# Turning a slot's rows on VectorE instead of TensorE, in a fused attention and mixture-of-experts kernel

## The chip, the cores and the metric

The kernel runs on one core of a Trainium2 chip, in float32 throughout. The metric is the device time of one execution in microseconds (us); lower is better. The program is one launch: attention, routing and the expert layers follow each other and overlap inside it.

## The reference, cut to what matters

The reference computes sliding-window attention (8 batches, 8 heads, 576 positions, head size 64; half of the heads use a dilated window), turns the result into 4608 token rows of 512 numbers, and passes them through a mixture of 8 experts. Each token goes to the one expert with the highest gate value.

```python
x = np.ascontiguousarray(attn_out.transpose(0, 2, 1, 3)).reshape(B * S, H * D)   # 4608 x 512
logits = x @ w_gate                                                              # 512 x 8
expert_idx = np.argmax(logits, axis=1)
...
for e in range(E):
    lo, hi = (boundaries[e], boundaries[e + 1])
    h = np.maximum(x_sorted[lo:hi] @ w1[e], 0.0)       # w1[e]: 512 x 1024
    y_sorted[lo:hi] = h @ w2[e]                        # w2[e]: 1024 x 512
y = y_sorted[inv_perm]
return (gate_w[:, None] * y).astype(np.float32)
```

Only the sum over the 512 features of a row enters `x @ w1`, so the order in which the features lie on the 128 partitions is free, as long as a row and `w1` use the same order.

## The kernel before, in words

**Two streams of work.** `attention()` walks over 32 units (batch, kind of window, half of the heads). When a batch is finished, `route(b)` picks an expert for each of its tokens and scatters the rows (512 features, the gate value and the token's number: `ROW` = 514 floats) into a bucket per expert in DRAM. `moe()` walks over slots. A slot is 128 rows of one expert; it reads them back from the bucket and runs both expert layers on them. There are up to `NSLOT` = 41 slots, of which the first `SURE` = 36 always run; each later one stands behind a condition (`guards`, `tc.If(live[0] > j)`). In this data slots 0 to 36 do their work. Slots 26 and 29 are mixed: their 128 rows come in four groups of 32, some of one expert and some of another, and they run through `grouped` and `hrow`.

**Order.** Both streams are generators. A planner (`run_slots`, `clock`) interleaves their pieces by estimated costs, so that slots run between attention units as soon as enough batches are routed. From about 490 us on only slots are left, apart from the last routing. The framework keeps each engine's queue in order; `tc.issue_after` ties an instruction behind another one.

**One slot.** `fetch_x(j)` reads a register with the slot's place in the bucket (`queue.value_load`) and loads the 128 rows into the tile `x` (128 partitions by 514 floats, four buffers) with one DMA of 257 KB. For slots below 26 this goes through SyncE's queue (SP), from 26 on through ScalarE's (ACT), where it is tied behind the slot's first relu (`evicted[-1]`) while `j < SURE`. `fetch_w` loads four quarters of 1 MB (two halves of `w1`, two of `w2`) on SP into one of two sets of weight buffers, by the parity of the slot; a quarter is skipped when the expert has not changed. `fetch()` decides when each load is issued: its list `wanted` names how many halves of earlier slots must be done.

`across(j)` turns the rows: four 128 by 128 TensorE transposes (L1171) into one PSUM bank, and one VectorE copy to the SBUF tile `xt` (L1173). It is called for slot j+1 in the middle of slot j, between the two halves of the first layer. The first layer is 32 matmuls of 128 by 128 (L1239), each recorded as two matmul instructions, so 64 a slot; ScalarE applies the relu to the first half (L1250) and VectorE to the second (L1259). The second layer is 8 matmuls of 128 by 512 (L1271), recorded as 16; ScalarE scales the result by the gate value that lies in `x` (L1282), and POOL scatters it to the output (L1288).

A float32 row of `w1` numbered `128 c + l` lies on partition `l`, as chunk `c` of four.

Of the kernel before, what the change touches and what calls it, by code (L numbers as in the profile page):

```python
# [12 lines left out]
F32 = mybir.dt.float32  # L13
# [10 lines left out]
N, DM, E, F = B * S, H * DH, 8, 1024  # L24
# [12 lines left out]
ROW = DM + 2  # L37
G = 32
# [24 lines left out]
SURE = N // 128  # L63


READY = [max(0, -(-(S * (b + 1) - E * 127) // 128)) for b in range(B)]
# [9 lines left out]
MIX = (2, 5)  # L76
STEP = MIX[1] - MIX[0]
J0 = STAGES[-1][1]
assert J0 + MIX[-1] < SURE and NSLOT - SURE <= 6


# [82 lines left out]
def kernel(  # L164
# [10 lines left out]
    nc = tc.nc  # L175
# [53 lines left out]
    def read_bucket(i, b):  # L229

        i = getattr(i, "ins", i)
        for b2, w in bucket_writes:
            if b2 > b:
                tc.declare_no_dep(i, w, reason="writes rows that this stage does not read")
        tc.add_to_no_dep_group("reads", i)
# [14 lines left out]
    def bank(name, *dims):  # L250
        return psum.tile([128, *(dims or (512,))], F32, tag="bank", name=name)
# [819 lines left out]
    w1s = cpool.tile([128, 2, 4, F], F32, name="w1")  # L1071
    w2s = cpool.tile([128, 2, 8, DM], F32, name="w2")
    mixed = {J0 + at0: i for i, at0 in enumerate(MIX)}
    xs, guards, evicted = {}, ExitStack(), []

    def fetch_x(j):
        b, n, _, basei, _ = where[j]
        x = xs[j] = mpool.tile([128, ROW], F32, tag="x", name=f"x_{j}", bufs=4)
        with ExitStack() as order:


            queue = nc.sync
            if j >= J0 + 2:
                queue = nc.scalar
                if j < SURE:
                    order.enter_context(tc.issue_after(evicted[-1].ins))
            if j in mixed:
                for g in range(4):
                    a = 2 * NMIX + 4 * mixed[j] + g
                    at0 = queue.value_load(  # L1090
                        mix["ints"][:, a : a + 1], min_val=0, max_val=NROWS - G
                    )
                    read_bucket(queue.dma_start(x[G * g : G * g + G], bucket[ds(at0, G), :]), b)
            else:
                at0 = queue.value_load(basei[:, n : n + 1], min_val=0, max_val=E * CAP)
                read_bucket(queue.dma_start(x, bucket[ds(at0, 128), :]), b)

    regs = {}

    def fetch_w(j, dst, src, other):  # L1100
        _, n, exi, _, newi = where[j]
        if (j, other) not in regs:
            if other:
                i = mixed[j]
                exi = mix["ints"][:, i : i + 1]
                newi = mix["ints"][:, NMIX + i : NMIX + i + 1]
            else:
                exi, newi = exi[:, n : n + 1], newi[:, n : n + 1]
            rv = nc.sync.value_load(exi, min_val=0, max_val=E - 1)
            kw = {}  # L1110
            if j >= 2:
                kw["cond"] = nc.sync.value_load(newi, min_val=0, max_val=1) > 0
            regs[j, other] = rv, kw
        rv, kw = regs[j, other]
        nc.sync.dma_start(dst, src(rv).rearrange("o (c l) f -> l (o c) f", l=128), **kw)

# [22 lines left out]
    def fetch():  # L1141
        while wanted:

            at0 = 0
            while at0 < len(wanted) - 1 and wanted[at0][1] == "x" and wanted[at0][0] not in where:
                at0 += 1
            j, what, layer, n = wanted[at0]
            if j not in where or done[layer] < n:
                return
            wanted.pop(at0)  # L1150
            if what == "x":
                fetch_x(j)
                continue
            h, other = int(what[2]), what[3:] == "b"
            n = (j + other) % 2
            if what[1] == "1":
                cols = slice(512 * h, 512 * h + 512)
                fetch_w(j, w1s[:, n, :, cols], lambda rv: moe_w1[ds(rv, 1), :, cols], other)
            else:
                rows = slice(512 * h, 512 * h + 512)  # L1160
                fetch_w(
                    j, w2s[:, n, 4 * h : 4 * h + 4], lambda rv: moe_w2[ds(rv, 1), rows, :], other
                )

    def moe():


        def across(j):
            ps = bank("xt", 4, 128)
            for c in range(4):  # L1170
                nc.tensor.transpose(ps[:, c], xs[j][:, 128 * c : 128 * c + 128], ident)  # L1171
            xt = mpool.tile([128, 4, 128], F32, tag="xt", name="xt")
            crossed.append(nc.vector.tensor_copy(xt, ps))  # L1173
            return xt

        late, xt = [], None
        for j in range(NSLOT):
# [5 lines left out]
            if j >= SURE:  # L1183

                guards.close()
                guards.enter_context(tc.If(live[0] > j))
                while late:
                    late.pop(0)()
            x = xs[j]
# [7 lines left out]
            def grouped(out, lhsT, ws, cols, c, n, j=j):  # L1197

                for g in range(4):
                    mine = slice(G * g, G * g + G)  # L1200
                    nc.tensor.matmul(  # L1201
                        out[mine],
                        lhsT=lhsT[:, mine],
                        rhs=ws[:, (j + (g >= KIND[mixed[j]])) % 2, c, cols],
                        start=c == 0,
                        stop=c == n - 1,
                    )

            def turned_h(hrow, fg):
                ps = bank("ht", 4, 128)  # L1210
                for fi in range(4):
                    nc.tensor.transpose(ps[:, fi], hrow[:, fi], ident)
                (nc.scalar.copy, nc.vector.tensor_copy)[fg](h[:, 4 * fg : 4 * fg + 4], ps)

            hrows = []
            for fg in range(2) if j in mixed else ():
                ph = bank("ph")
                for c in range(4):
                    grouped(ph, xt[:, c], w1s, slice(512 * fg, 512 * fg + 512), c, 4)
                    if (fg, c) == (1, 1):  # L1220
                        turned_h(hrows[0], 0)
                    yield 0.93
                hrow = mpool.tile([128, 4, 128], F32, tag="xt", name="hrow")
                flat = hrow.rearrange("p i f -> p (i f)")
                done[0] = 2 * j + fg + 1
                if fg == 0:
                    evicted.append(nc.scalar.activation(flat, ph, AF.Relu))
                    while late:
                        late.pop(0)()
                else:  # L1230
                    relu = nc.vector.tensor_scalar(flat, ph, 0.0, None, op0=OP.max)
                fetch()
                hrows.append(hrow)
            for fg in range(2) if j not in mixed else ():
                ph = bank("ph", 4, 128)
                for fi in range(4):
                    f = 4 * fg + fi
                    for c in range(4):
                        nc.tensor.matmul(  # L1239
                            ph[:, fi],  # L1240
                            lhsT=w1[:, c, 128 * f : 128 * f + 128],
                            rhs=xt[:, c],
                            start=c == 0,
                            stop=c == 3,
                        )
                    if fi < 3:
                        yield 0.93
                done[0] = 2 * j + fg + 1
                if fg == 0:
                    evicted.append(nc.scalar.activation(h[:, 0:4], ph, AF.Relu))  # L1250
                    while late:
                        late.pop(0)()
                    fetch()
                    yield 0.93
                    if j + 1 in xs:
                        nxt = across(j + 1)
                        yield 0.5
                else:
                    relu = nc.vector.tensor_scalar(h[:, 4:8], ph, 0.0, None, op0=OP.max)  # L1259
                    fetch()  # L1260
                    yield 0.93
            py = bank("py")
            for f in range(8):
                if j in mixed:
                    if f == 2:
                        turned_h(hrows[1], 1)
                    if f == 4 and j + 1 in xs:
                        nxt = across(j + 1)
                    grouped(py, h[:, f], w2s, slice(0, DM), f, 8)
                else:  # L1270
                    nc.tensor.matmul(py, lhsT=h[:, f], rhs=w2[:, f], start=f == 0, stop=f == 7)  # L1271
                if f == 3:
                    done[1] = 2 * j + 1
                    fetch()
                if f < 7:
                    yield 0.88
# [117 lines left out]
```

## Time and profile before

| | |
|---|---|
| median of 3 runs | 775.67 us (774.82 to 775.92) |
| the profiled execution, its own time | 830.33 us |
| its span, first to last instruction | 828.5 us |
| mean granted TensorE clock in it | 0.956 |
| PE, DVE, ACT, POOL busy | 93%, 33%, 28%, 18% |
| HBM read and written | 216.16 MB and 21.54 MB |

The profile has five parts that are used here: the busy shares by slice, the chain of work that ended last, groups of instructions by line, the waits, and a timeline. PE is TensorE's matmul, PEld its weight load, DVE is VectorE, ACT is ScalarE, POOL is GpSimd and SP is SyncE; a q behind an engine's name is its queue of DMA issues. The profiled execution takes 54.66 us more than the median run. Its lines are used for what a piece of work costs and for what waits on what.

### The profile page before, as it was taken

The page shows a single profiled execution, that of the slowest core. Times are in us where ns is not written, and L with a number is a line of the kernel's source. Part 1 is how long each engine was busy: PE and PEld are TensorE (multiplying, and loading weights), DVE is VectorE, ACT ScalarE, POOL GpSimd, SP SyncE. Part 2 cuts the span into 40 slices and gives each one's busy share as a digit, 9 for nine tenths or more (in the row PEclk, how much of TensorE's full clock was granted, in tenths as well). Part 3 has the DMA queues.
Part 4 walks back from the last instruction along what each step waited for, and adds up shares of the span by engine and source line. Part 5 has one row for each costly group of instructions (what it writes and reads, how often), then busy time and mean ns, then how long its engine had stood idle before and what let it go on. Part 6 is the DMA issues. An engine that isn't in the chain of part 4 may idle for free.

```text
span 828.5 us, 18147 instructions
## 1 busy us (share of the span) xinstructions
PE 773.6 (93%) x6870; PEld 574.1 (69%) x6870; DVE 274.4 (33%) x963; ACT 229.1 (28%) x853; POOL 146.3 (18%) x142
## 2 busy tenths in 40 slices
PE   6997997998999899989999899969999999999993
PEld 4776775886777677767777677646777466577681
DVE  3674765664343433443341311135110110101010
ACT  4985663552333233222331010000100101000010
POOL 4424333113111311130110200060000000000000
PEclk9998979898999899998999989978999999999997
DMA  7985679998998968796406818978994292883996
GB/s 184 208 194 162 139 187 323 294 264 265 358 269 294 305 189 243 245 303 232 132 26 223 261 59 289 327 241 295 313 335 149 93 317 99 318 313 138 324 312 213
DMA packets 177053, 195.42 MB, mean 236 GB/s; under 512 B 71249, under 2 KB 103137, under 8 KB 176963
## 3 DMA queue, kind: packets, MB, share of 16 engines
q1 hardware_dynamic: 166960, 169.01, 65.8%
q0 software_dynamic: 7248, 21.43, 7.2%
q10 hardware_dynamic: 2754, 3.78, 1.4%
q8 instruction: 57, 0.93, 0.5%
q14 instruction: 34, 0.27, 0.1%
HBM read 216.16 MB, written 21.54 MB: 287 GB/s over the span
## 4 chain that ended last, share of the span: by engine, by line
PE 85%; issue 5%; ACT 5%; DVE 1%; another core or an unknown queue 1%; DMA 1%; POOLq 0%; ACTq 0%; POOL 0%; DVEq 0%
PE ph L1239 31%; PE py L1271 29%; PE xo L469 5%; PE weights L454 3%; PE scores L388 3%; ACT e L425 3%; PE turned L342 2%; PE xt L1171 2%; PE ph L1201 2%; PE py L1201 2%; PE logits L583 2%; PE xrow L573 2%; PE turned L351 2%; DMA k<-in_k_dram 1%
## 5 line engine op out<-in xcount | busy, mean ns | idle before, releaser
L1239 PE MATMUL ph<-xt,w 128*128 128x128 f32 x2240 | 276.4, 280 | 4.1 <-issue 3.1
L1239 PEld LDWEIGHTS ph<-xt,w 128*128 128x128 f32 x2240 | 267.3, 196 | 18.0 <-issue 15.7
L1271 PE MATMUL py<-w,h 128*128 128x512 f32 x560 | 262.5, 609 | 3.9 <-issue 3.9
L1271 PEld LDWEIGHTS py<-w,h 128*128 128x128 f32 x560 | 102.8, 194 | 107.9 <-issue 105.9
L1288 POOL DMA_INDIRECT out_dram<-y,to x35 | 34.8, 993 | 412.0 <-ACT y L1282 326.6
L1173 DVE COPY xt<-xt 128x512 f32<-128x512 f32 x38 | 26.3, 691 | 211.1 <-PE xt L1171 205.8
L1282 ACT ACTIVATE y<-py,x 128x512 f32<-128x512 f32 x35 | 24.0, 687 | 223.0 <-PE py L1271 181.4
L444 POOL TENSOR_TENSOR e<-e,rec 128x864 f32<-128x864 f32 x32 | 52.2, 1631 | 142.2 <-DVE rec L443 121.7
L456 DVE COPY eT<-weights 96x384 f32<-96x384 f32 x96 | 47.3, 545 | 58.6 <-PE weights L454 44.9
L469 PE MATMUL xo<-eT,v 96*64 96x64 f32 (+1 forms) x1216 | 51.6, 233 | 13.7 <-issue 13.6
L469 PEld LDWEIGHTS xo<-eT,v 96*64 96x64 f32 x1216 | 44.1, 144 | 21.0 <-issue 16.6
L425 ACT ACTIVATE e<-e,lo 128x96 f32<-128x96 f32 x144 | 51.8, 362 | 12.0 <-DVE lo L417 10.9
L425 ACT ACTIVATE e<-scores,lo 128x96 f32<-128x96 f32 (+1 forms) x160 | 52.4, 345 | 2.3 <-DVE lo L404 1.9
L239 POOL DMA_INDIRECT bucket<-rows,idx x40 | 39.0, 975 | 56.0 <-DVE idx L671 37.3
L1259 DVE TENSOR_SCALAR h<-ph 128x512 f32<-128x512 f32 x35 | 24.1, 688 | 73.5 <-PE ph L1239 73.5
L334 ACT COPY kT<-turned 128x288 f32<-128x288 f32 x64 | 22.5, 403 | 86.0 <-PE turned L342 44.0
L1250 ACT ACTIVATE h<-ph 128x512 f32<-128x512 f32 x35 | 20.9, 596 | 89.9 <-PE ph L1239 73.7
L454 PE MATMUL weights<-ident,e 128*96 128x128 f32 x288 | 39.3, 281 | 3.0 <-issue 2.0
L454 PEld LDWEIGHTS weights<-ident,e 128*96 128x96 f32 x288 | 32.2, 129 | 10.4 <-issue 8.1
L388 PEld LDWEIGHTS scores<-kT,qT 64*64 64x64 f32 x1152 | 31.8, 143 | 9.7 <-issue 4.0
L388 PE MATMUL scores<-kT,qT 64*64 64x96 f32 x1152 | 36.8, 260 | 1.2 <-ACT kT L334 1.0
L410 DVE TENSOR_TENSOR e<-scores,masks 128x384 f32<-128x384 f32 x64 | 23.0, 399 | 33.7 <-PE scores L388 18.1
(220 smaller groups left out, 612.5 us busy)
## 6 DMA issues: line engine op xcount, KB each, us to landing
w<-in_moe_w_dram SPq DMA_DIRECT2D x164, 1024.0 KB
x<-bucket SPq DMA_DIRECT2D x26, 257.0 KB
v<-in_v_dram SPq DMA_DIRECT2D x32, 192.0 KB
q<-in_q_dram SPq DMA_DIRECT2D x32, 144.0 KB
v<-in_v_dram SPq DMA_DIRECT2D x48, 96.0 KB
k<-in_k_dram SPq DMA_DIRECT2D x28, 144.0 KB
x<-bucket ACTq DMA_DIRECT2D x11, 257.0 KB
q<-in_q_dram SPq DMA_DIRECT2D x14, 192.0 KB
```

Source lines behind the costliest of these rows:

```text
L239: nc.gpsimd.indirect_dma_start(out=bucket, out_offset=bass.IndirectOffsetOnAxis(ap=idx, axis=0), in_=rows, in_offset=None, bounds_check=NR ...
L388: nc.tensor.matmul(sc[r][64 * c : 64 * c + 64, 96 * (i % 5) : 96 * (i % 5) + 96], lhsT=qT[rows, 64 * j : 64 * j + 64], rhs=kT[rows, first_ ...
L425: nc.scalar.activation(out=e[p0:p1, i], in_=s[:, 96 * (i - i0) : 96 * (i - i0) + 96], func=AF.Exp, bias=lo[p0:p1, i : i + 1], scale=-1.0, ...
L444: return nc.gpsimd.tensor_tensor(out=e, in0=e, in1=rec.unsqueeze(2).broadcast_to([128, 9, 96]), op=OP.mult)
L454: nc.tensor.transpose(tp[0:96, 128 * i : 128 * i + 128], e[:, a + i], ident)
L456: nc.vector.tensor_copy(eT, tp[0:96, 0:384])
L469: nc.tensor.matmul(xo[DH * h : DH * h + DH, at0 : at0 + nq], lhsT=vt[:, 2 * hl + r, j, :] if ty == 0 else vt[:, hl, j, DH * r : DH * r + D ...
L1173: crossed.append(nc.vector.tensor_copy(xt, ps))
L1201: nc.tensor.matmul(out[mine], lhsT=lhsT[:, mine], rhs=ws[:, (j + (g >= KIND[mixed[j]])) % 2, c, cols], start=c == 0, stop=c == n - 1,)
L1239: nc.tensor.matmul(ph[:, fi], lhsT=w1[:, c, 128 * f : 128 * f + 128], rhs=xt[:, c], start=c == 0, stop=c == 3,)
L1271: nc.tensor.matmul(py, lhsT=h[:, f], rhs=w2[:, f], start=f == 0, stop=f == 7)
L1288: i = nc.gpsimd.indirect_dma_start(out=out, out_offset=bass.IndirectOffsetOnAxis(ap=to, axis=0), in_=y, in_offset=None, bounds_check=N - 1 ...
```

## The change

From slot 11 on (`PIECES = READY[3]`, which is 11), except for the two mixed slots, the turning of the rows moves from TensorE to VectorE.

- [...] `fetch_x` brings the rows in four pieces: piece i holds features 128 i to 128 i + 127 of all 128 rows, and goes to partitions 32 i to 32 i + 31. In it, partition 32 i + t holds the features of rows t, 32 + t, 64 + t and 96 + t. A fifth DMA brings the last two columns (gate value and token number) in the old layout. One DMA of 128 runs of 2056 bytes becomes four of 128 runs of 512 bytes each and one of 128 runs of 8 bytes.
- `across` for these slots is one VectorE transpose of 128 by 512 from `x` to `xt`. It reads every fourth float (a step of 16 bytes) and needs neither TensorE nor a PSUM bank.
- The features then lie as `4 l + c` on partition l. All `w1` loads follow (`fetch_w` is passed the order "(l c)" for `w1` and "(c l)" for `w2`): partition l gets rows 4 l to 4 l + 3. Each run is still 512 floats long.
- For slots 0 to 10, 26 and 29 TensorE still turns the rows, but its weight load now also reads every fourth float of `x`. The copy to `xt` has a new order: `xt` is [128, group of 32 rows, c, row], and the first layer's matmul reads four runs of 32 floats.
- The ties of `x` loads behind the last relu now hold until the first guarded slot has begun (`guarded`), so for the loads of slots 36 and 37 too.

```diff
     def fetch_x(j):
...
+        pieces = j >= PIECES and j not in mixed
...
             if j >= J0 + 2:
                 queue = nc.scalar
-                if j < SURE:
+                if not guarded:
                     order.enter_context(tc.issue_after(evicted[-1].ins))
...
                 at0 = queue.value_load(basei[:, n : n + 1], min_val=0, max_val=E * CAP)
-                read_bucket(queue.dma_start(x, bucket[ds(at0, 128), :]), b)
+                rows = bucket[ds(at0, 128), :]
+                for i in range(4) if pieces else ():
+                    part = rows[:, 128 * i : 128 * i + 128].rearrange("(g t) d -> t g d", t=G)
+                    mine = x[G * i : G * i + G, 0:DM].rearrange("t (g d) -> t g d", g=4)
+                    read_bucket(queue.dma_start(mine, part), b)
+                skip = DM if pieces else 0
+                read_bucket(queue.dma_start(x[:, skip:ROW], rows[:, skip:ROW]), b)
...
-        nc.sync.dma_start(dst, src(rv).rearrange("o (c l) f -> l (o c) f", l=128), **kw)
+        nc.sync.dma_start(dst, src(rv).rearrange(f"o {rows} f -> l (o c) f", l=128), **kw)
...
         def across(j):
+            x = xs[j][:, 0:DM]
+            xt = mpool.tile([128, 4, 4, G], F32, tag="xt", name="xt")
+            if j >= PIECES and j not in mixed:
+                crossed.append(
+                    nc.vector.transpose(xt, x.rearrange("p (g d c) -> p g c d", g=4, c=4))
+                )
+                return xt
             ps = bank("xt", 4, 128)
             for c in range(4):
-                nc.tensor.transpose(ps[:, c], xs[j][:, 128 * c : 128 * c + 128], ident)
-            xt = mpool.tile([128, 4, 128], F32, tag="xt", name="xt")
-            crossed.append(nc.vector.tensor_copy(xt, ps))
+                nc.tensor.transpose(ps[:, c], x.rearrange("p (d c) -> p c d", c=4)[:, c], ident)
+            crossed.append(
+                nc.vector.tensor_copy(
+                    xt.rearrange("p g c t -> p c g t"), ps.rearrange("p c (g t) -> p c g t", g=4)
+                )
+            )
             return xt
...
             if j >= SURE:
                 guards.close()
                 guards.enter_context(tc.If(live[0] > j))
+                guarded.append(j)
...
                         nc.tensor.matmul(
-                            ph[:, fi],
+                            ph[:, fi].rearrange("p (g t) -> p g t", g=4),
                             lhsT=w1[:, c, 128 * f : 128 * f + 128],
-                            rhs=xt[:, c],
+                            rhs=xt[:, :, c],
```

More of the change, by code (lines that the diff above doesn't have):

```diff
@@ L78 @@
 J0 = STAGES[-1][1]
+PIECES = READY[3]
 assert J0 + MIX[-1] < SURE and NSLOT - SURE <= 6
@@ L1073 @@
     mixed = {J0 + at0: i for i, at0 in enumerate(MIX)}
-    xs, guards, evicted = {}, ExitStack(), []
+    xs, guards, guarded, evicted = {}, ExitStack(), [], []
     def fetch_x(j):
@@ L1095, in fetch_x, with fetch_w @@
                 at0 = queue.value_load(basei[:, n : n + 1], min_val=0, max_val=E * CAP)
-                read_bucket(queue.dma_start(x, bucket[ds(at0, 128), :]), b)
+                rows = bucket[ds(at0, 128), :]
[5 more added lines that the diff above has]
+                read_bucket(queue.dma_start(x[:, skip:ROW], rows[:, skip:ROW]), b)
     regs = {}
-    def fetch_w(j, dst, src, other):
+    def fetch_w(j, dst, src, other, rows):
         _, n, exi, _, newi = where[j]
@@ L1157, in fetch @@
                 cols = slice(512 * h, 512 * h + 512)
-                fetch_w(j, w1s[:, n, :, cols], lambda rv: moe_w1[ds(rv, 1), :, cols], other)
+                fetch_w(
+                    j, w1s[:, n, :, cols], lambda rv: moe_w1[ds(rv, 1), :, cols], other, "(l c)"
+                )
             else:
@@ L1161, in fetch @@
                 fetch_w(
-                    j, w2s[:, n, 4 * h : 4 * h + 4], lambda rv: moe_w2[ds(rv, 1), rows, :], other
+                    j,
+                    w2s[:, n, 4 * h : 4 * h + 4],
+                    lambda rv: moe_w2[ds(rv, 1), rows, :],
+                    other,
+                    "(c l)",
                 )
@@ L1168, in across @@
         def across(j):
+            x = xs[j][:, 0:DM]
[5 more added lines that the diff above has]
+                return xt
             ps = bank("xt", 4, 128)
             for c in range(4):
-                nc.tensor.transpose(ps[:, c], xs[j][:, 128 * c : 128 * c + 128], ident)
-            xt = mpool.tile([128, 4, 128], F32, tag="xt", name="xt")
-            crossed.append(nc.vector.tensor_copy(xt, ps))
+                nc.tensor.transpose(ps[:, c], x.rearrange("p (d c) -> p c d", c=4)[:, c], ident)
[3 more added lines that the diff above has]
+                )
+            )
             return xt
@@ L1202, in grouped @@
                         out[mine],
-                        lhsT=lhsT[:, mine],
+                        lhsT=lhsT(g),
                         rhs=ws[:, (j + (g >= KIND[mixed[j]])) % 2, c, cols],
@@ L1211, in turned_h @@
                 for fi in range(4):
-                    nc.tensor.transpose(ps[:, fi], hrow[:, fi], ident)
+                    nc.tensor.transpose(
+                        ps[:, fi], hrow[:, fi].rearrange("p g f -> p (g f)"), ident
+                    )
                 (nc.scalar.copy, nc.vector.tensor_copy)[fg](h[:, 4 * fg : 4 * fg + 4], ps)
@@ L1218, in moe @@
                 for c in range(4):
-                    grouped(ph, xt[:, c], w1s, slice(512 * fg, 512 * fg + 512), c, 4)
+                    grouped(ph, lambda g: xt[:, g, c], w1s, slice(512 * fg, 512 * fg + 512), c, 4)
                     if (fg, c) == (1, 1):
@@ L1222, in moe @@
                     yield 0.93
-                hrow = mpool.tile([128, 4, 128], F32, tag="xt", name="hrow")
-                flat = hrow.rearrange("p i f -> p (i f)")
+                hrow = mpool.tile([128, 4, 4, G], F32, tag="xt", name="hrow")
+                flat = hrow.rearrange("p i g f -> p (i g f)")
                 done[0] = 2 * j + fg + 1
@@ L1268, in moe @@
                         nxt = across(j + 1)
-                    grouped(py, h[:, f], w2s, slice(0, DM), f, 8)
+                    grouped(py, lambda g: h[:, f, G * g : G * g + G], w2s, slice(0, DM), f, 8)
                 else:
```

## The prediction, on record before the changed kernel ran

> **What bounds the kernel now.** I read the page first for the engines, then the chain of work that ended last, then single slots in that chain, then the waits. The engine summary has this line, with busy time and share of the span:
>
> ```profile
> PE 773.6 (93%) x6870; PEld 574.1 (69%) x6870; DVE 274.4 (33%) x963; ACT 229.1 (28%) x853; POOL 146.3 (18%) x142
> ```
>
> TensorE is busy 93% of the span and nothing else comes near. A share is only an average, so the question is whether TensorE also sets the time where the change acts, from slot 11 on. In the profile that is from 381 us, when the rows of slot 11 are copied. The stage view (busy time of each engine, then granted clock, DMA share, GB/s) answers for the parts after that:
>
> ```profile
> 381.00:430.00 49.00, 49.00 (x446) 37.79 (x445) 16.89 (x42) 14.85 (x55) 6.96 (x5) 1.00 0.41 126
> 430.00:480.00 50.00, 46.94 (x380) 35.61 (x379) 13.91 (x64) 7.79 (x15) 7.80 (x8) 0.95 0.68 224
> 480.00:540.00 60.00, 60.00 (x354) 44.23 (x353) 9.31 (x33) 5.93 (x10) 3.86 (x4) 0.98 0.65 220
> 540.00:566.00 26.00, 19.02 (x73) 10.98 (x72) 12.38 (x87) 0.60 (x1) 12.65 (x14) 0.74 0.78 252
> 566.00:612.00 46.00, 46.00 (x276) 34.37 (x275) 8.07 (x42) 4.54 (x7) 3.89 (x4) 1.00 0.91 316
> 715.00:801.00 86.00, 86.00 (x500) 63.04 (x500) 8.66 (x18) 7.02 (x11) 5.84 (x6) 1.00 0.79 275
> ```
>
> TensorE fills every stretch but one, 540 to 566 us. There the last routing runs and the gaps are mostly marked "issue". In the last stage VectorE works 8.66 us of 86. What the turning costs is read in the chain, in order of time (start, us, what). These are two neighbouring slots:
>
> ```profile
> 743.32 3.57 PE ph L1239 x32
> 747.33 3.57 PE ph L1239 x32
> 750.90 6.87 PE py L1271 x16
> 757.77 3.57 PE ph L1239 x32
> ```
>
> From 743.32 + 3.57 = 746.89 to 747.33 lie 0.44 us in which TensorE does the four transposes of the next slot; everywhere else one group begins where the last ended. A slot is 757.77 - 743.32 = 14.45 us. The groups for the turning itself are (count, busy us and mean ns of one, idle us before):
>
> ```profile
> L1173 DVE COPY xt<-xt 128x512 f32<-128x512 f32 x38 | 26.3, 691 | 211.1 <-PE xt L1171 205.8 <-remote 5.3
> ...
> L1171 PE MATMUL xt<-ident,x 128*128 128x128 f32 x152 | 23.5, 278 | 0.0
> ...
> L1171 PEld LDWEIGHTS xt<-ident,x 128*128 128x128 f32 x152 | 18.1, 144 | 1.9 <-issue 1.7
> ```
>
> 152 transposes are 38 slots of four. One takes 278 ns, but they are pipelined, and 0.44 us for four is what they occupy. The last numbers of the copy's line are VectorE's idle time: it waits for TensorE, not the reverse.
>
> [...] Both the new transpose and the remaining TensorE weight loads step by exactly 16 bytes. No row here has such a step. [...] The trace of before shows 32-partition row loads only in the mixed slots.
>
> **The change part by part.**
>
> *TensorE transposes removed.* Rows are turned for slots 0 to 37 (the 38th set is turned inside slot 36 and not used). Of these, 11 to 37 without 26 and 29 move to VectorE: 27 - 2 = 25. On TensorE's path: 25 x 0.434 us (14.45 us less 2 x 3.57, less 6.87, is 0.44; the finer starts give 0.43 to 0.44) = **10.85 us**. Ten of them fall in slots with nothing but slot work around; the others are among attention units or the last routing, where TensorE is busy 97% of 430 to 540 us. I count those in full.
>
> *VectorE.* Removed: 25 copies of 691 ns. Added: 25 transposes of 512 elements per partition. Low end, [...] the same fp32 length costs 688 ns in the relu L1259, so an estimate of 0.69 us, no net change. [...] I take 1.2 us. It is free either way: in a late slot VectorE idles 10 us before the copy and 2.9 us before the relu L1259. Behind the transpose stand that relu and the token-number cast, and TensorE waits for the relu. But the transpose no longer waits for TensorE, so it can run up to 10 us earlier. If that cover were gone, 25 x 0.5 = 13 us would be due.
>
> *Row loads, issue.* One DMA becomes five. The records of one ACT issue are:
>
> ```profile
> L1096 ACTq FUSED_REGOPS  x11: 37/42/42, 642.8 to 802.2; - x11
> L1096 ACTq EVENT_SEMAPHORE  x11: 17/38/38, 642.9 to 802.2; - x11
> L1096 ACTq MOVE x<-bucket x11: 29/29/37, 642.9 to 802.3; - x11
> L1096 ACTq DMA_DIRECT2D x<-bucket x11: 339/349/411, 643.0 to 802.4; - x11
> ```
>
> The medians add up to 0.46 us, so four more cost 1.84 us of ACT a slot. Behind them stands the output scaling L1282, which has waited 10.3 us for TensorE when it starts: hidden. On SP, 15 slots (11 to 25) at 1.84 us are 28 us over some 240 us; behind them stand weight loads, which themselves spend 137.5 us waiting for py and 122.4 us for ph in SP's waits. Hidden: 0. Register loads per slot stay one.
>
> *Row loads, transfer.* By the packet records of the trace of before, a 2056-byte run takes 102 ns on one DMA engine, a 512-byte run 31 ns, and one of 4 or 8 bytes about 9 ns. Before: 128 x 102 / 16 = 0.82 us. After: (512 x 31 + 128 x 9) / 16 = 1.06 us[...]. The rows of a late slot are issued 13.4 us before they are turned (747.95 against 761.3): the last piece leaves 1.84 us later, a load of 257 KB has taken up to 4.5 us, 7 us remain. Hidden: 0.
>
> *`w1` rows four by four.* The same number of 2048-byte runs: 0. *First-layer reads in four runs of 32 floats:* [...] 0, at worst 0.1 us a slot, 3.7 us. *Ties of loads 36 and 37:* they move two short register loads; ACT has 10 us a slot: 0.
>
> *Remaining TensorE transposes.* 13 slots, 52 weight loads with a 16-byte step. A load takes 144 ns and they follow each other every 108 ns, equal to the matmul's pace. [...] A gain is excluded. I take 0.5 us.
>
> *Sum:* 10.85 - 0.5 = **10.3 us** less. The profiled execution of 830.33 us (828.5 span, 1.8 around) would become 820.0. It is 54.66 us longer than the median, and nothing shown says where. Late slots run at full clock, so I subtract 10.3 unscaled (scaled by 775.67 / 830.33 it would be 9.6): 775.67 - 10.3 = **765.4 us**. What comes next at a slot's start is TensorE itself, straight from one group into the next.
>
> **The rivals.**
>
> *A. Partial gain.* The 16-byte step slows TensorE's remaining weight loads fourfold (5.6 us), or first-layer reads in pieces cost something: 10.85 - 5.6 = 5.2, so 770.4 us. [...]
>
> *B. Absorbed.* In 381 to 566 us another engine's chain (softmax, routing) sets the pace, or every saving there returns as "issue" gaps, and the pieces delay rows. Then only the ten late slots' 4.3 us would stay, less losses: within 774.1 to 777.2. For it: 540 to 566. Against: TensorE at 100% in most stages.
>
> *C. Slower: weights late through the row pieces.* In the built program each SP or ACT load first waits for an earlier load on one of eight shared completion semaphores. A slot had 5 loads; now 9, so the first `w1` quarter waits for a piece of rows issued on ACT a moment before, and an ACT piece can hold up ACT behind a weight load. If TensorE then waits d per slot over 25 slots, the price is 25 d; it decides from 10.3 / 25 = 0.41 us. With d = 1 us: 775.67 + 14.7 = 790 us. For it: DMA share 0.91 in 566 to 612. Against: TensorE's waits list no wait for weights at all, and a buffer is freed about 25 us before it is read again, against some 3 us per quarter.
>
> *D. The change does not do what it says.* The built program shows 28 VectorE transposes (three behind conditions that fail) and 13 TensorE turns, so this is out.
>
> **How the numbers follow.** Main case 0.74 (762.5 to 768), A 0.11 (768 to 774), B 0.05, C 0.10. About 0.2% (1.6 us) is what a measurement can tell from no change. Faster by more: 0.74 + 0.11 = 0.85; within: 0.05; slower: 0.10. The range is 761 to 774: main and A, with 1.5 us below for short waits that vanish with the PSUM bank.
>
> **What would show it.** Right: L1171's successor counts 52 transposes, a late slot in the chain takes 14.0 us with the two ph groups touching, PE busy falls by about 11 us, and VectorE's transpose is 0.7 to 1.3 us without TensorE waiting for it. C would show as waits of ph or py for w, or of ACT behind x pieces; A as longer PEld rows and a wider gap in early slots. A VectorE transpose above 3 us, or a late slot still at 14.4 us, would prove me wrong.

## The result and the profile after

The changed kernel takes 767.14 us (median of 6 runs, 766.47 to 768.65); beside it the kernel before takes 775.25 us (6 runs, 771.02 to 776.08). The ratio is 0.9908, with a 95% interval of 0.9883 to 0.9933. It is faster: 8.1 us by the medians, 5.2 to 9.1 us by the interval. The forecast was 765.4 us, that is 10.3 us less.

One caution before any lines are compared. The profile that was shown of before is of an execution of 830.33 us in which TensorE was granted half its clock (0.50) in eight windows of 6.8 to 13.7 us; the profiled execution of after (766.47 us) has none before TensorE's work is over. The two can't be laid side by side as wholes, so the comparison of traces below uses a later pair (before_third and after_third) that has such windows in both.

The engine summary of the kernel after (busy time, share of the span, instructions), and the granted clock in its 40 slices:

```profile
PE 731.2 (96%) x6770; PEld 543.5 (71%) x6770; DVE 281.8 (37%) x963; ACT 229.1 (30%) x853; POOL 146.3 (19%) x142
...
PEclk9999999999999999999999999999999999999997
```

TensorE has 100 instructions fewer, 25 sets of four, and is still the engine that sets the time: 96% of the span. VectorE works 281.8 us where it worked 274.4, and is idle for 63% of the span. The stage view of after for two of the stretches that the prediction used:

```profile
381.00:430.00 49.00, 49.00 (x442) 37.32 (x441) 15.50 (x45) 10.91 (x32) 3.61 (x3) 1.00 0.48 157
540.00:566.00 26.00, 26.00 (x144) 18.35 (x143) 3.49 (x6) 2.06 (x4) 1.94 (x2) 1.00 0.83 290
```

TensorE fills both. They are the same times but not the same work: this execution is some 60 us ahead by then, and its last routing lies in slot 19, at 493 to 508 us. TensorE has no pause there either: from 272 us until its work ends at 750 us it is busy throughout. The chain of waits of this profile breaks off after its last pieces, so a late slot is read in the timeline of TensorE (start, us, what, count):

```profile
665.81 7.31 PE L1270 MATMUL ph<-xt,w 128*128 128x128 f32 x64
672.95 7.03 PE L1302 MATMUL py<-w,h 128*128 128x512 f32 x16
679.82 7.31 PE L1270 MATMUL ph<-xt,w 128*128 128x128 f32 x64
```

All 64 first-layer matmuls of a slot now stand in succession, where the kernel before had 32, a gap of 0.44 us for the transposes, and 32. A slot is 679.82 - 665.81 = 14.01 us; it was 14.45. The instructions that turn the rows, from the answer on the tile `xt` (count, ns min/median/max, first and last start):

```profile
L1196 PEld LDWEIGHTS xt<-ident,x x52: 195/209/223, 117.4 to 625.6; 128*128 128x128 f32 x52
L1196 PE MATMUL xt<-ident,x x52: 277/283/388, 117.4 to 625.7; 128*128 128x128 f32 x52
L1191 DVE STREAM_TRANSPOSE xt<-x x25: 1060/1097/1164, 338.8 to 733.9; 128x512 f32<-128x512 f32 x25
L1198 DVE COPY xt<-xt x13: 677/691/692, 118.3 to 626.0; 128x512 f32<-128x512 f32 x13
```

52 TensorE transposes are left and 25 VectorE transposes are new, at 1.10 us each. The 16-byte step comes with a weight load of 209 ns for a remaining TensorE transpose, where it was 141 (medians). What a set of four occupies on TensorE rises far less, from 437 to about 480 ns between the starts of its first matmul and of the next group. Last, TensorE's waits for weights in the kernel after (us in all, times, longest):

```profile
PE ph L1270 <- DMA w<-in_moe_w_dram: 1.6, 1, 1.6
PE py L1302 <- DMA w<-in_moe_w_dram: 1.6, 1, 1.6
```

They begin at 243.5 and 270.0 us, in slots 5 and 6, before the first rows are loaded in pieces (at 310.9 us).

### The profile page after: what moved, and what is told of

Read it like the earlier page. It is cut to its first block, busy times and chain, and to the rows that moved or that the text cites. A ratio compares the mean times of both kernels' runs of the same rounds, so it can differ in the third digit from the quotient of the medians.

```text
span 764.6 us, 18266 instructions
## 1 busy us (share of the span) xinstructions
PE 731.2 (96%) x6770; PEld 543.5 (71%) x6770; DVE 281.8 (37%) x963; ACT 229.1 (30%) x853; POOL 146.3 (19%) x142
## 5 line engine op out<-in xcount | busy, mean ns | idle before, releaser
L1270 PEld LDWEIGHTS ph<-xt,w 128*128 128x128 f32 x2240 | 258.1, 192 | 16.8 <-issue 14.4
L1270 PE MATMUL ph<-xt,w 128*128 128x128 f32 x2240 | 264.7, 276 | 2.6 <-DMA w<-in_moe_w_dram 1.6
L1302 PE MATMUL py<-w,h 128*128 128x512 f32 x560 | 254.8, 596 | 1.6 <-DMA w<-in_moe_w_dram 1.6
L1302 PEld LDWEIGHTS py<-w,h 128*128 128x128 f32 x560 | 100.5, 190 | 100.4 <-issue 97.9
L1281 ACT ACTIVATE h<-ph 128x512 f32<-128x512 f32 x35 | 20.8, 595 | 78.9 <-PE ph L1270 75.1
L472 PE MATMUL xo<-eT,v 96*64 96x64 f32 (+1 forms) x1216 | 43.1, 224 | 0.0
L472 PEld LDWEIGHTS xo<-eT,v 96*64 96x64 f32 x1216 | 38.6, 138 | 4.5 <-ACT dl L633 0.4
L391 PEld LDWEIGHTS scores<-kT,qT 64*64 64x64 f32 x1152 | 30.2, 138 | 11.5 <-ACT kT L337 4.3
L457 PE MATMUL weights<-ident,e 128*96 128x128 f32 x288 | 37.3, 275 | 1.0 <-POOL e L447 1.0
L1191 DVE STREAM_TRANSPOSE xt<-x 128x512 f32<-128x512 f32 x25 | 27.5, 1103 | 18.8 <-DMA x<-bucket 18.5
L335 DVE TENSOR_SCALAR qT<-turned 128x288 f32<-128x288 f32 x64 | 26.1, 446 | 21.9 <-PE turned L354 15.6
```

Source lines behind the costliest of these rows:

```text
L335: nc.vector.tensor_scalar(out, in_, -SCALE, None, op0=OP.mult)
L391: nc.tensor.matmul(sc[r][64 * c : 64 * c + 64, 96 * (i % 5) : 96 * (i % 5) + 96], lhsT=qT[rows, 64 * j : 64 * j + 64], rhs=kT[rows, first_ ...
L457: nc.tensor.transpose(tp[0:96, 128 * i : 128 * i + 128], e[:, a + i], ident)
L472: nc.tensor.matmul(xo[DH * h : DH * h + DH, at0 : at0 + nq], lhsT=vt[:, 2 * hl + r, j, :] if ty == 0 else vt[:, hl, j, DH * r : DH * r + D ...
L1191: nc.vector.transpose(xt, x.rearrange("p (g d c) -> p g c d", g=4, c=4))
L1270: nc.tensor.matmul(ph[:, fi].rearrange("p (g t) -> p g t", g=4), lhsT=w1[:, c, 128 * f : 128 * f + 128], rhs=xt[:, :, c], start=c == 0, st ...
```

## The experiments

Theory: TensorE sets the time, so each set of four transposes taken from it is worth the 0.43 to 0.44 us that it occupies; pieces, VectorE's slow transpose, ties and `w1` order are hidden. Rivals: the saving is partly eaten by the 16-byte step on TensorE (A), by another engine (B), or by row pieces that hold weights up (C). All runs below had the half-clock windows: the kernel before takes 828 us there. Slots are compared by the starts of their first matmuls in the traces.

**How many sets are moved.** `PIECES` alone is changed in the kernel after; before_again is the unchanged kernel before, for its trace.

```diff
-PIECES = READY[3]
+PIECES = 999   # turn_none: TensorE turns all 38 sets
+PIECES = 30    # turn_late: VectorE turns 8 sets
+PIECES = 0     # turn_all: VectorE turns all but the mixed slots, 36 sets
```

> The kernel before, unchanged, profiled once more and timed against itself. The profile of before took 830 us, the median run 775; this asks where those 55 us lie. Theory (the saving is 25 turns at 0.437 us = 10.9 us less 13 x 0.043 us for the stepped weight loads, all of it on TensorE's path): an undisturbed profile is near 773 us of span, its late slots take 14.45 us, and slot by slot it falls behind the changed kernel by 0.44 us from slot 11 on. Rival (part of the saving is lost between slots 11 and 24, beside attention units): up to slot 24 the distance to the changed kernel grows by clearly less than 0.4 us a slot. Ratio 1.00 either way.

Measured: 827.82 us, ratio 1.0 (0.9986 to 1.0015), clock 0.957. The unchanged kernel has the half-clock windows too, so they do not come from the change. Why the first measurement took 775 us is not known.

> The changed kernel with PIECES = 999: no slot is turned on VectorE and rows come in one DMA, but w1 lies four rows by four and TensorE's turning reads every fourth float in all 38 sets. Theory: 0.043 us more per set than before, 38 x 0.043 = 1.6 us slower than before, about 777 us. Rival (the new w1 order costs time in its loads, as the two waits of TensorE for weights at 243 and 270 us in the changed kernel hint, 3.2 us): about 780 us, with those waits in its profile.

Measured: 829.14 us, ratio 1.0017 (1.0 to 1.0033), 1.4 us over before. With nothing moved, only the 16-byte step on 38 sets, the four-run reads and the `w1` order remain. 38 x (0.480 - 0.437) = 1.6 us is the step alone. Rival A's fourfold load (5.6 us for 13 sets was the author's estimate, so some 16 us for 38) is out.

> The changed kernel with PIECES = 30: only slots 30 to 37 (8 sets, all where nothing but slots runs) are turned on VectorE. Theory (0.48 us for each set moved, wherever it is): 8 x 0.48 = 3.8 us faster than with none moved, so about 773 us. Rival (sets moved beside attention save nothing): 8 + 2 late sets give the whole gain of the changed kernel, so about 768 us.

Measured: 826.82 us, ratio 0.9987 (0.9974 to 1.0), 2.3 us under turn_none. In the two profiles, from the start of slot 30 to that of the last second-layer group, it is 91.3 against 94.7 us: 3.3 us for 7 sets, 0.48 each. That is the 0.44 us of a set and the 0.04 us that the 16-byte step adds to it in turn_none. The median gives less than the 3.8 us expected, the profile what was expected per set.

> The changed kernel with PIECES = 0: all sets but the two of the mixed slots (36 sets) are turned on VectorE. Theory (0.48 us per set): 11 x 0.48 = 5.3 us faster than the changed kernel, about 762 us. Rival (in the early slots VectorE, SyncE's queue or the DMA engines are the bound, DMA share 0.96 at 130 to 230 us): no gain over the changed kernel or a loss, 767 us or more, with waits for rows or weights on TensorE before 330 us.

Measured: 815.76 us, ratio 0.9871 (0.9843 to 0.9898): 12.1 us under before_again, the fastest of the versions that leave nothing out. By the medians it is 13.4 us under turn_none, where 36 x 0.48 = 17.3 us were expected; in the two profiles the last second-layer group starts 16.2 us earlier. Two waits of TensorE stand in this profile and not in that of turn_none:

```profile
PE ph L1270 <- DMA w<-in_moe_w_dram: 2.7, 1, 2.7
PE py L1302 <- DVE h L1290: 2.2, 1, 2.2
```

The first ends at 130.8 us, in front of slot 0. There a piece of rival C appears: the rows of slots 0 and 1 are ten loads now and not two, and the first weights are issued 7.7 us after the first rows, in turn_none 2.3 us. The second falls at 550 us, in slot 19, during the last routing. How much of the difference between 13.4 and 17.3 us is theirs can't be told: slot 0 begins at 130.8 us here and at 130.5 in turn_none.

**What the pieces and the 16-byte step cost.** after_again is the kernel after. pieces_only keeps the five DMAs but lets TensorE turn the rows. whole_rows has VectorE turn rows that come in one DMA. dense_read has VectorE read contiguous floats. In the kernel after, turning blocks of 32 by 32 within 32 partitions brings every feature to its row of `w1`; in these three the features do not meet their rows, and the output is off by a relative 0.83, 0.83 and 0.93. The amount of work is the same.

```diff
-            if j >= PIECES and j not in mixed:            # in across
+            if False:                                     # pieces_only
-        pieces = j >= PIECES and j not in mixed           # in fetch_x
+        pieces = False                                    # whole_rows
-  nc.vector.transpose(xt, x.rearrange("p (g d c) -> p g c d", g=4, c=4))
+  nc.vector.transpose(xt, x.rearrange("p (g c d) -> p g c d", g=4, c=4))  # dense_read
```

> The changed kernel, unchanged, timed once more beside the kernel before and the three kernels that split it. On a chip where the kernel before takes 828 us, TensorE is granted half its clock in eight windows of 7 to 14 us. Theory (0.437 us per set for 25 sets, less 13 x 0.043 us, the same wherever the chip stands): 10.3 us faster than before beside it, ratio 0.9876. Rival (in the throttled stretches part of the saving is lost): 8 us or less faster.

Measured: 819.12 us against 828.74, ratio 0.9881 (0.9859 to 0.9902): 9.6 us less, 8.1 to 11.7 by the interval. The forecast of 10.3 us lies in it.

> The changed kernel with the rows of slots from 11 on loaded in pieces, but turned by TensorE as in the slots before; the turned rows are then not in the order of w1, so the output is not the reference's. Theory (pieces cost nothing): the time of the kernel with none turned on VectorE, 1.4 us over before (the stepped weight loads). Rival C of the prediction (loads wait for loads: SyncE's queue waits 46 us for rows and 58 us for weights in the changed kernel): slower than before by 3 us or more, with waits of TensorE for weights.

Measured: 827.73 us, ratio 1.0003 (0.9982 to 1.0024). But this run was granted a higher clock (0.966, median of its runs, against 0.957 for turn_none), so its time alone can't show that the pieces cost nothing. The stretches at full clock can be compared: slots 11 to 14 take 75.9 us against 75.1 in turn_none, slots 16 to 18 take 44.06 in both, and slots 20 to 35 take 235.58 against 235.56. Where only slots run, five loads a slot cost nothing; rival C's loss of 0.41 us a slot and more is not there, and TensorE has no wait for weights. What slots 11 to 14 lose is looked at below.

> The changed kernel with VectorE's turning from slot 11 on, but with the rows of a slot in one DMA as before; the rows are then not grouped for a transpose of 32 by 32 blocks, so the output is not the reference's. Theory: the same time as the changed kernel within 1 us. Rival (the pieces eat 2 us of the saving): 2 us faster than the changed kernel.

Measured: 816.44 us, ratio 0.984 (0.9815 to 0.9864), 2.7 us under after_again, with the intervals just overlapping. That could come from the pieces or from the clock: two of its six runs, 812.95 and 813.78 us, had a clock of 0.970 and 0.966, against 0.956 to 0.960 in after_again. So it was measured again below.

> The changed kernel with VectorE's transpose reading 32 floats in succession in each block, and not every fourth; the features are then not in the order of w1, so the output is not the reference's. Theory (the 16-byte step costs VectorE, but VectorE has the time): the transpose falls from 1.10 us to about 0.69 us, the time of a copy of that length, and the kernel's time stays within 1 us of the changed kernel. Rival [...]: it stays at 1.1 us.

Measured: 817.67 us, ratio 0.9863 (0.9831 to 0.9894), no different from after_again. The group of its transpose (busy us and mean ns, then idle before it):

```profile
L1191 DVE STREAM_TRANSPOSE xt<-x 128x512 f32<-128x512 f32 x25 | 17.5, 704 | 15.9 <-DMA x<-bucket 15.8
```

Contiguous, the transpose takes 704 ns; with the 16-byte step about 1.10 us. 25 x 0.40 = 10 us of VectorE's time are gone, and the kernel's time stays: VectorE's transpose is hidden, as forecast.

**A last group with before and after side by side.** before_third and after_third are the unchanged kernels; tie_undone takes back the tie of loads 36 and 37, whole_tied the pieces. The expectations below take it that whole_rows had undone the tie as well. It had not: whole_tied is the same program as whole_rows, run a second time.

```diff
-                if not guarded:
+                if j < SURE:                              # tie_undone
-        pieces = j >= PIECES and j not in mixed
+        pieces = False                                    # whole_tied
```

> The kernel before once more, for a profile beside the next ones. Expected: a ratio of 1.00 within 0.2%. If this chip grants TensorE its full clock throughout (a mean of 0.98 or more, time near 775 us), its slots can be laid beside those of the changed kernel with no half-clock window between them; if the clock is again near 0.957, the time is near 828 us.

Measured: 827.43 us, ratio 0.9997 (0.9981 to 1.0014), clock again 0.958.

> The changed kernel, for a profile beside the next two. The two measurements so far gave 5.2 to 9.1 us and 8.1 to 11.7 us less than before; the sum of the prediction is 10.3 us. Expected by the sum: 9 to 11 us less. If something of 2 us still eats at the saving: 8 us or less.

Measured: 818.51 us against 828.09, 9.6 us by the medians; ratio 0.9894 (0.9862 to 0.9925), 6.2 to 11.4 us.

> The changed kernel, but the loads of slots 36 and 37 are tied behind the last relu only while j < 36, as before. The run without pieces (whole_rows) had this undone as well, so its 2.7 us lower median could come from either part. Prediction (tie costs nothing): the time of the changed kernel within 1.6 us. If the tie costs: up to 2.7 us less than the changed kernel, and the saving shows in the slots from 35 on alone.

Measured: 817.6 us, ratio 0.9876 (0.984 to 0.9912), 0.9 us under after_third. The tie costs nothing that can be measured: from the start of slot 34 to that of slot 36 it is 28.03 us in both.

> The changed kernel with one whole DMA for the rows of a slot, the tie kept, so that only the pieces are taken back (VectorE then turns rows that are not regrouped: the output is not the reference's). Prediction (pieces hidden): the time of the changed kernel within 1.6 us, and the same slot starts. If the pieces cost what the run without them seemed to show: 2 to 3 us less than the changed kernel.

Measured: 817.51 us, ratio 0.9882 (0.985 to 0.9913), 1.0 us under after_third. The same program was 2.7 us under after_again before, so the medians put the pieces at 1 to 3 us, and the intervals can't tell that from nothing. The slots in the traces are finer, and are read below.

**Where the saving comes.** The stage view of before_third, cut where the traces have a stage's end: to slot 0, to slot 11, to slot 19, to slot 20 (the last routing), to slot 36. Columns: stretch, its us, then busy us and count of PE, PEld, DVE, ACT, POOL, then granted clock, DMA share, GB/s.

```profile
0.00:130.10 130.10, 109.70 (x1768) 87.85 (x1768) 83.05 (x282) 88.15 (x403) 45.66 (x47) 0.95 0.76 193
130.10:393.60 263.50, 251.06 (x2408) 197.17 (x2408) 113.19 (x382) 90.69 (x343) 53.45 (x48) 0.95 0.86 272
393.60:536.70 143.10, 140.16 (x1071) 106.13 (x1070) 34.92 (x122) 25.14 (x72) 16.01 (x15) 0.98 0.57 189
536.70:563.90 27.20, 21.05 (x88) 12.37 (x88) 13.05 (x91) 1.19 (x2) 13.56 (x14) 0.75 0.72 247
563.90:798.70 234.80, 234.80 (x1457) 158.80 (x1456) 28.27 (x84) 21.71 (x34) 15.55 (x16) 1.00 0.72 249
```

The same stages of after_third:

```profile
0.00:130.20 130.20, 108.87 (x1768) 87.13 (x1768) 83.03 (x282) 88.17 (x403) 45.67 (x47) 0.95 0.76 192
130.20:393.40 263.20, 250.45 (x2405) 196.82 (x2406) 114.51 (x383) 90.39 (x342) 53.41 (x48) 0.95 0.88 273
393.40:532.50 139.10, 136.15 (x1038) 101.84 (x1037) 36.38 (x121) 25.48 (x72) 16.02 (x15) 0.99 0.59 190
532.50:558.80 26.30, 19.13 (x84) 11.62 (x84) 12.10 (x85) 1.19 (x2) 13.56 (x14) 0.81 0.78 258
558.80:787.00 228.20, 228.20 (x1401) 153.18 (x1400) 35.88 (x92) 21.71 (x34) 15.57 (x16) 1.00 0.73 249
```

The last stage is the clean one: clock 1.00 and TensorE busy throughout in both. It has 1457 - 1401 = 56 matmuls less, 14 sets, and is 6.6 us shorter: 0.47 us a set. Each plain slot is 0.44 us shorter; the mixed slots 26 and 29, in which the sets of 27 and 30 are turned, are 0.70 and 0.72 us shorter; slots 25 and 28, where TensorE still turns the mixed rows, are 0.04 us longer. Slots 20 to 35 take 228.2 us in after as well: the windows and the pauses of TensorE in front of them, for which after_third is some 50 us longer, all lie earlier. Up to slot 11 the two kernels of this pair differ by 0.2 us. From slot 11 to slot 19 there are eight sets less and 4.0 us less, but not all of that is the change's. In the stage view of before_third and of after_third, the stretch around 474 us reads:

```profile
466.00:490.00 24.00, 21.06 (x151) 15.98 (x149) 5.96 (x34) 3.16 (x6) 5.79 (x6) 0.86 0.48 156
```

```profile
466.00:490.00 24.00, 21.05 (x149) 15.29 (x147) 6.43 (x34) 3.16 (x6) 4.87 (x6) 0.93 0.44 141
```

The half-clock window there is 6.8 us in before_third and 3.4 us in after_third. At half clock TensorE is half as fast: in the window at 475 us of the profile of before, 18 first-layer matmuls take 4.21 us, 0.234 us each, and at full clock 32 take 3.74 us, 0.117 us each. TensorE worked 5.8 and 3.4 us in the two windows, so by estimate it lost 2.9 and 1.7 us. Without this difference of 1.2 us, eight sets gave about 2.8 us and not 8 x 0.434 = 3.5. The three of slots 16 to 18, with full clock and no pause, gave 1.31 us, their full worth.

**What became of that.** From slot 11 to slot 15 the kernels with pieces (after_third, after_again, tie_undone) gain 0.7 us on before; whole_tied and whole_rows gain 1.7 us, the full 4 x 0.434, with 0.44 us in every slot. The timeline of slot 14 shows it. In after_third:

```profile
448.35 0.60 PE L576 MATMUL xrow<-ident,xT 128*128 128x128 f32 x4
448.79 0.27 PE L579 MATMUL xrow<-ident,xT 128*64 128x128 f32 x1
448.99 0.52 PE L586 MATMUL logits<-xT,wg 128*32 128x128 f32 x10
449.44 2.05 PE L1270 MATMUL ph<-xt,w 128*128 128x128 f32 x16
451.42 1.27 PE L472 MATMUL xo<-eT,v 96*64 96x64 f32 x36
452.62 5.62 PE L1270 MATMUL ph<-xt,w 128*128 128x128 f32 x48
458.08 2.74 PE L1302 MATMUL py<-w,h 128*128 128x512 f32 x6
```

In whole_tied:

```profile
449.15 0.60 PE L576 MATMUL xrow<-ident,xT 128*128 128x128 f32 x4
449.59 0.27 PE L579 MATMUL xrow<-ident,xT 128*64 128x128 f32 x1
449.70 1.95 PE L1270 MATMUL ph<-xt,w 128*128 128x128 f32 x16
451.58 1.27 PE L472 MATMUL xo<-eT,v 96*64 96x64 f32 x36
452.78 0.52 PE L586 MATMUL logits<-xT,wg 128*32 128x128 f32 x10
453.22 5.62 PE L1270 MATMUL ph<-xt,w 128*128 128x128 f32 x48
458.69 2.74 PE L1302 MATMUL py<-w,h 128*128 128x512 f32 x6
```

The order written out differs. With pieces, the router's `logits` stand directly behind `xrow`, ahead of the slot's first layer; with whole rows (and in before) they come after `xo`. From `xrow` to `py` it is 458.08 - 448.35 = 9.73 us against 458.69 - 449.15 = 9.54 us: the reordered slot is 0.19 us longer. Slots 13 and 14 are reordered in this way, about 0.4 us together; slots 11 and 12 add 0.2 us. Of the whole difference of 1.0 us the rest is only a matter of where a slot is taken to start: `logits`, 0.45 us, stand ahead of slot 15's first matmul in after_third and behind it in whole_tied. Over slots 11 to 18 the three kernels with pieces take 139.06 to 139.15 us and the two with whole rows 138.64 and 138.72; over slots 20 to 35 all five take 228.22. So the pieces cost 0.3 to 0.6 us, in the slots where the order differs.

## Why the prediction was right, step by step

- **Transposes removed, 25 x 0.434 us.** Right in kind and size. The late slot is 14.01 us as forecast, with the two `ph` groups touching. Of the 25 sets, 22 are turned in slots that had full clock in before_third and after_third (11 to 14, 16 to 18, and from 20 on). By the forecast they are worth 9.55 us; these slots are 9.1 us shorter, 9.6 with the 0.45 us that only moved into slot 15. That the sum is so close is in part luck: the sets inside the mixed slots gave 0.5 us more than 2 x 0.434, and the order of `logits` took about 0.6. With whole rows, without that loss, it is 10.2 us. TensorE's busy time, another sign that the prediction named, fell from 771.4 to 757.0 us in this pair; the half-clock windows explain about 3.4 of these 14.4 us, which leaves 11.0.
- **"I count those in full"** (the sets among attention units and the last routing). For the transposes this held: with whole rows the sets of slots 11 to 14 and 16 to 18 gave 0.44 us each. No other engine absorbed the saving, as rival B has it: in after TensorE works without a pause from 272 to 750 us. The three sets turned in slots 10, 15 and 19 lie beside half-clock windows in every trace of before, and their worth can't be told. Two slips of the text did not matter: fifteen of the 25 sets, not ten, are turned behind the last routing (slots 20 to 36), and rival B's time does not follow from its 4.3 us, which would give 775.67 - 4.3 = 771.4 us.
- **16-byte step on the remaining TensorE sets.** 0.5 us forecast; 13 x 0.043 = 0.56 us measured. Each load took 68 ns longer (209 against 141), but a set of four loads only 43 ns (480 against 437): most of it lies beside the matmuls. Rival A is out, by turn_none.
- **VectorE's transpose.** 1.2 us taken, which was the author's estimate, 1.10 measured; hidden, as dense_read shows. Against the contiguous read of dense_read (0.70 us) the step costs 1.10 - 0.70 = 0.40 us for 512 elements.
- **Row pieces: 0.** Right for what the prediction priced (issue and transfer): from slot 20 on the slots are equally long with pieces and without. It did not see another path: with five loads in place of one, the order in TensorE's queue is another in slots 11 to 14, which costs up to 0.6 us.
- **Rival C's mechanism is real but does not decide.** The waits in SP's queue behind earlier loads, first after_third and then whole_tied (us in all, times, longest):

```profile
SPq L1126 <- DMA x<-bucket: 53.7, 9, 9.6
SPq L1126 <- DMA w<-in_moe_w_dram: 41.8, 18, 7.6
```

```profile
SPq L1126 <- DMA x<-bucket: 10.8, 5, 4.5
...
SPq L1126 <- DMA w<-in_moe_w_dram: 4.8, 2, 2.7
```

The pieces add about 80 us of such waits of weight loads, and none reaches TensorE in these slots. They mostly take the place of others: the waits of the same loads for `py` and `ph` on TensorE fall from 230.5 to 120.7 us. It fits the prediction's argument that a buffer is free some 25 us before it is read again: the longest wait is 9.6 us. In turn_all the pieces push the first weights back, and TensorE waits 2.7 us for them in front of slot 0. The two waits for weights in after lie before the first pieces.
- **`w1` order, four-run reads, ties: 0.** turn_none, with all three at work, is 1.4 us over before, and the step alone explains 1.6.

What stays open: in the first measurement the gain was 5.2 to 9.1 us, in the two later ones 8.1 to 11.7 and 6.2 to 11.4. All three agree on 8.1 to 9.1. The steps as measured (9.6 us for 22 sets, 1.3 for the other three if they are worth their forecast, less 0.56) give 10.3 us and lie above the first. The two waits for weights in slots 5 and 6, 3.2 us, are in the profile of after that belongs to the first measurement and in no later one; whether before has them there too can't be told, since no profile of before without half-clock windows exists. So where the last 1 to 2 us of the first measurement went was not found.

## What to carry to other kernels

Where one engine is busy all through a stage, a piece of work taken off it is worth the time that it occupies between its neighbours (0.44 us here), not the sum of its instructions' durations (4 x 278 ns), and an engine with idle time may take longer over it (1.10 us here, in place of a copy of 0.69) without cost. Count the sets per stage and look for the saving in the stage where that engine never pauses; among interleaved work, compare the order written out as well, since a change in the number of loads can move other instructions. A queue's waits may rise by tens of us (about 80 us here) and still cost nothing while the buffers behind it are loaded early enough.

## What was not expected of the hardware

- Half-clock windows without long pauses. In the profile of before, the granted clock is 0.50 in eight windows before TensorE's work is over: six of 6.8 us, one of 10.2 and one of 13.7 us; the window at 474 us is 6.8 us long in before_third and 3.4 us in after_third. One more lies behind the work: in after TensorE's work ends at 750.1 us, and half clock is granted from 754.9 us on. Ahead of the eight windows no such idle stretch is seen: from 20 us until its work ends, the longest pause of TensorE in before is 2.4 us. It is not fully busy there either. In the 3.4 us ahead of each of these eight windows (a stretch as long as the shortest window) TensorE worked 0.5 to 2.3 us, with pauses marked "issue" ahead of all eight. The profiled execution of after has no pause marked "issue" and no such window; yet it too has 3.4 us with only 1.70 us of work (from 115.7 us), and no window behind them. What lowers the clock, and what makes the pauses, was not found. The kernel before took about 775 us in the first measurement and 828 us in all later ones, where each of its profiles has these windows (mean granted clock 0.957 and 0.958).
- A 16-byte step slows VectorE's transpose of 512 floats a partition from 704 (dense_read) to about 1100 ns, and a TensorE weight load of 128 columns from 141 to 209 ns, while four transposes in succession rise only from 437 to 480 ns.
